# State steps of 64 tokens from chunk 6 on, with k and v loaded by head parity over the partitions

**Chip, cores, metric.** One core of one Trainium2 chip. Times are device microseconds (us) of a whole execution. Most executions of one kernel agree within 1%; some are disturbed and are marked "slow", and comparisons use fast runs alone. The engines: PE is TensorE (PEld its weight loads), DVE VectorE, ACT ScalarE, POOL GpSimd, SP SyncE. A "q" behind a name (SPq) means the engine's instruction queue, which issues DMAs.

## The reference

Linear attention with decay over 4 batches, 8 heads, 768 tokens, head size 64, in blocks of 64 tokens; then an MLP (512 to 2048 to 512) over the 3072 tokens.

```python
Dmask = np.where(rel >= 0, lam[:, None, None] ** rel[None], 0.0)
for b in range(nb):                                  # blocks of 64 tokens
    intra = einsum('bhic,bhjc->bhij', qb, kb) * Dmask
    intra = einsum('bhij,bhjd->bhid', intra, vb)
    inter = einsum('bhid,bhde->bhie', qb * lam_pow, kv_state)
    out[:, :, sl] = intra + inter
    kv_state = lam_block * kv_state + einsum('bhsd,bhse->bhde', kb * rev_pow, vb)
# x: out with the heads side by side, (3072, 512)
h = x @ w_in
g = where(h >= 1, h, where(h <= -1, 0, (h + 1)**2 / 4))
return g @ w_out
```

## The kernel before

A chunk `c` is 128 tokens of one batch with all 8 heads (`C` = 128, `HP` = 4 head pairs, `D` = 64), so there are 24. Six MLP stages of four chunks each follow the attention. PE's two MLP products take most of the time; the attention's work is laid between them.

The order of every engine's instructions is fixed when the program is built: each operation is declared with `add(key, engine, ns, function, needs, due)`, and a list scheduler places them by these assumed durations. At run time each engine then goes through its own list in order.

The operations of one chunk that the change touches:

```python
def f_load(c, x):                      # x: 0 q, 1 k, 2 v; 256 KB, one DMA
    t = qkv_ld[c, x] = ld.tile([128, H, D], F32, ...)      # 6 buffers each
    e = nc.gpsimd if (c, x) > (0, 1) and c < SW else nc.sync
    d = e.dma_start(out=t, in_=(q, k, v)[x][b, :, s0:s0 + C, :].rearrange("h p d -> p h d"))
    ...
def f_xt(c):                           # k and q transposed by the DMA's crossbar
    nc.sync.dma_start_transpose(out=t..., in_=qk[c]...)
def cast_v(c):                         # v times its decay, to bf16
    nc.gpsimd.tensor_tensor(vn[c % NV]..., qkv_ld[c, 2], _bc(tab_k[:, c % NCB, :], 2, D), op=AX.mult)
def f_vb(c, g, hi):                    # v made block-diagonal: 4 small DMAs a chunk
    (nc.gpsimd if c < VP else nc.sync).dma_start(out=vi[c % NV][HD[hi], :, g, hi, :], in_=vn[c % NV][HD[g], :, hi, :])
def f_kb(c, hi):                       # k^T made block-diagonal: 2 DVE copies
    ...nc.vector.tensor_copy(kbd[c % NKB][HD[hi], :, :, hi, :], ptt[c][HD[hi], 0]...)
def f_u(c):                            # state += k^T v, 128 tokens at once
    for hp in range(HP):
        nc.tensor.matmul(pu[0][:, hp, :], lhsT=pair(ks[c], hp), rhs=vn[c % NV][:, hp]..., ...)
def f_s(c, g):                         # scores: 128 columns for g = 0, 64 for g = 1
    ...nc.tensor.matmul(pst[c, g][:, hp, :], lhsT=kbd[c % NKB][:, hp, g]..., rhs=qT[c][:, hp, 64 * g:], ...)
# the load as the scheduler knows it (sp: on the SyncE queue):
add(key, "SP" if sp else "POOL", 600 if sp and i == 0 else 1050 if sp else 900 ..., fn, need, due=0, ...)
```

Of the kernel before, what the change touches and what calls it, by code (L numbers as in the profile page):

```python
# [23 lines left out]
def kernel(  # L24
# [31 lines left out]
    PLAIN, KA = 4, 1  # L56
    LD, RING = 6, 6
# [6 lines left out]
    NQK, NXT, XT = 4, 2, 8  # L64
    qkp = ctx.enter_context(tc.tile_pool(name="qkp", bufs=NQK))
# [37 lines left out]
    NKB, NUB, NV = 3, 3, 4  # L103
    kbd = [const.tile([128, HP, 2, 2, D], BF16, name=f"kbd{i}") for i in range(NKB)]
    ubd = [const.tile([128, HP, 128], BF16, name=f"ubd{i}") for i in range(NUB)]
    vi = [const.tile([128, HP, 2, 2, D], BF16, name=f"vi{i}") for i in range(NV)]
    vn = [const.tile([128, HP, 2, D], BF16, name=f"vn{i}") for i in range(NV)]
# [17 lines left out]
    causal = const.tile([128, 128], F32)  # L125
    plain = const.tile([128, 128], F32)
    for t, p in ((plain, pos[:, 0:1]), (causal, late)):
        nc.vector.tensor_tensor(t, row[:, 0:128], _bc(p, 1, 128).rearrange("p a b -> p (a b)") if False else p.to_broadcast([128, 128]), op=AX.is_ge)
# [11 lines left out]
    tab_k = const.tile([128, NCB, H], F32)  # L140
    tab_q = const.tile([128, NCB, HP, 128], F32)
# [5 lines left out]
    const.tile([128, 56], F32, name="pad1")  # L147
# [28 lines left out]
    def run_plan(free):  # L176
# [25 lines left out]
        while len(out_seq) < len(ops):  # L202
# [4 lines left out]
            if e == "DVE" and t < pool_end:  # L207
                if x.key[0] == "g1" or x.key[0] == "kb" and x.key[1] >= XT:
                    ns += pool_end - t
                elif x.key[0] in ("g2", "g"):  # L210
                    ns += min(ns, (pool_end - t) / 2)
# [5 lines left out]
            for u in users[x.key]:  # L217
                left[u.key] -= 1
                if left[u.key] == 0:
                    lat = SLACK if u.eng == "PE" and x.end > 30000 else DSLACK if u.eng == "SP" else LAT  # L220
                    rel = o_due(u.key[1]) - (14000 if u.key[0] == "t" else 18000) if u.key[0] in ("t", "xt") and u.key[1] >= CPS else o_due(u.key[1]) - 30000 if u.key[0] == "li" and u.key[1] > SW else 0
                    ready[u.eng].append((max([rel] + [y.t if y.eng == u.eng else y.end + lat for y in u.needs]), u))
# [16 lines left out]
    qk, qs, ks, qT, sc_sb, xT, ptt, pst, pot = {}, {}, {}, {}, {}, {}, {}, {}, {}  # L239
# [6 lines left out]
    def cast(c, x, e):  # L246
        if c not in qk:
            qk[c] = qkp.tile([128, 2, H, D], BF16, name="qk", tag="qk")
            ks[c], qs[c] = qk[c][:, 0], qk[c][:, 1]
        t = qk[c][:, 1 - x]  # L250
        if e == "ACT":
            nc.scalar.copy(out=t, in_=qkv_ld[c, x])  # L252
        else:
            nc.vector.tensor_tensor(t, qkv_ld[c, x], qkv_ld[c, x], op=AX.max)

    def f_xt(c):
        t = xtp.tile([128, 2, HP, 128], BF16, name="xq", tag="xq")
        ptt[c] = t
        nc.sync.dma_start_transpose(out=t.rearrange("p a h k -> p (a h) k"), in_=qk[c].rearrange("p a h d -> p (a h d)"))

    def cast_v(c):
        nc.gpsimd.tensor_tensor(vn[c % NV].rearrange("p a b d -> p (a b) d"), qkv_ld[c, 2],  # L262
                                _bc(tab_k[:, c % NCB, :], 2, D), op=AX.mult)

    VP = 24

    def f_vb(c, g, hi):
        o, i = vi[c % NV][HD[hi], :, g, hi, :], vn[c % NV][HD[g], :, hi, :]
        (nc.gpsimd if c < VP else nc.sync).dma_start(out=o, in_=i)  # L269

# [6 lines left out]
    def f_kb(c, hi):  # L277
        if c < PLAIN:
            (nc.scalar.copy if c < KA else nc.vector.tensor_copy)(out=kplain(c), in_=ptt[c][:, 0])
        else:  # L280
            nc.vector.tensor_copy(kbd[c % NKB][HD[hi], :, :, hi, :], ptt[c][HD[hi], 0].rearrange("p a (b d) -> p a b d", b=2))

    def kplain(c):
        return kbd[c % NKB][:, 0:2].rearrange("p a b c d -> p (a b c d)").rearrange("p (h k) -> p h k", k=128)
# [5 lines left out]
    def f_u(c):  # L290
        if c % NCB == 0:
            pu[0] = pp_u.tile([128, HP, 128], F32, name="pu", tag="pu")
        for hp in range(HP):
            nc.tensor.matmul(pu[0][:, hp, :], lhsT=pair(ks[c], hp), rhs=vn[c % NV][:, hp].rearrange("p a d -> p (a d)"),  # L294
                             start=(c % NCB == 0 and hp == 0), stop=True, skip_group_check=True)

    def f_ub(c, hi):
        nc.scalar.copy(out=ubd[c % NUB][HD[hi], :, HD[hi]], in_=pu[0][HD[hi], :, HD[hi]])  # L298

    def f_s(c, g):  # L300
        t = pp_s.tile([128, 4, 128], F32, name="ps", tag="ps")
        pst[c, g] = t if g == 0 or c < PLAIN else t[:, 0:2, :].rearrange("p a (b d) -> p (a b) d", b=2)
        for i in range(4 if c < PLAIN else 0):
            nc.tensor.matmul(t[:, i, :], lhsT=kplain(c)[HD[g], i, :], rhs=qT[c][HD[g], i, :], start=True, stop=True)
        for hp in range(HP if c >= PLAIN else 0):
            nc.tensor.matmul(pst[c, g][:, hp, :], lhsT=kbd[c % NKB][:, hp, g].rearrange("p a d -> p (a d)"),  # L306
                             rhs=qT[c][:, hp, 64 * g:], start=True, stop=True)

    def f_m(c, g):
        if c < PLAIN:  # L310
            t = scp.tile([128, HP, 128], BF16, name="sc128", tag="sc128")
            sc_sb[c] = sc_sb.get(c, []) + [t]
            nc.vector.tensor_tensor(t, pst[c, g], _bc(plain, 1, HP), op=AX.mult)
            return
        if g == 0:
            sc_sb[c] = [scp.tile([128, HP, n], BF16, name=f"sc{n}", tag=f"sc{n}") for n in (128, 64)]
        nc.vector.tensor_tensor(sc_sb[c][g], pst[c, g], _bc(causal[:, 0:128 - 64 * g], 1, HP), op=AX.mult)  # L317

    def f_o(c):
        cb = c % NCB  # L320
        po = pot[c] = pp_o.tile([128, HP, 128], F32, name="po", tag="po")
        for hp in range(HP):
            if cb > 0:
                nc.tensor.matmul(po[:, hp], lhsT=ubd[(c - 1) % NUB][:, hp, :], rhs=qT[c][:, hp, :],  # L324
                                 start=True, stop=False)
            for hi in range(2 if c < PLAIN else 0):
                nc.tensor.matmul(po[HD[hi], hp], lhsT=vn[c % NV][:, hp, hi, :], rhs=sc_sb[c][hi][:, hp, :],
                                 start=(cb == 0), stop=True)
            for g in range(2 if c >= PLAIN else 0):
                nc.tensor.matmul(po[:, hp, 64 * g:], lhsT=vi[c % NV][:, hp, g].rearrange("p a d -> p (a d)"),  # L330
                                 rhs=sc_sb[c][g][:, hp, :], start=(cb == 0 and g == 0), stop=(g == 1))
# [66 lines left out]
    T0, STEP, LEAD = 24000, 1015, 3000  # L398
# [25 lines left out]
    def f_load(c, x):  # L424
        t = qkv_ld[c, x] = ld.tile([128, H, D], F32, name=f"x{x}f", tag=f"x{x}f")
        b, s0 = c // NCB, (c % NCB) * C
        e = nc.gpsimd if (c, x) > (0, 1) and c < SW else nc.sync
        d = e.dma_start(out=t, in_=(q, k, v)[x][b, :, s0:s0 + C, :].rearrange("h p d -> p h d"))  # L428
        if c == SW and x == 1:
            tc.add_manual_dep(d.ins, w_dma[7].ins.name, SYNC)  # L430

    SW = 7
    order = [("c", 0), ("c", 1), ("w", 0), ("c", 2), ("w", 1), ("c", 3), ("w", 2), ("w", 3), ("c", 4), ("w", 4), ("w", 5), ("w", 6), ("c", 5), ("c", 6), ("w", 7)]
    order += [("c", c) for c in range(7, NCH)]

    fifo, landed, splast = [], [], []
    for kind, i in order:
        for x in (1, 0, 2) if kind == "c" else (0,):
            sp = kind == "c" and not (0 < i < SW or (i, x) == (0, 2))
            if kind == "w":  # L440
                key, land, ns, fn, need = ("wi", i), ("w", i), 2800, lambda i=i: load_w(i), []
            else:
                key, land, ns, fn = ("li", i, x), ("ld", i, x), 1060 if sp else 720 if i < 2 else 800, lambda i=i, x=x: f_load(i, x)
                need = [("cast", i - LD, x), ("w", 7) if i == SW else None]
# [7 lines left out]
            add(key, "SP" if sp else "POOL", 600 if sp and i == 0 else 1050 if sp else 900 if kind == "c" else 800, fn, need, due=0, extra=1250 if sp else 930)  # L452
# [3 lines left out]
    for i in range(NKB):  # L456
        last = max(c for c in range(PLAIN) if c % NKB == i)
        add(("z", "kb", i), "DVE", 485, lambda i=i: nc.vector.memset(flat(kbd[i]), 0.0), [("s", last, 1)])
    for i in range(NV):
        add(("zv", i), "POOL", 530, lambda i=i: nc.gpsimd.memset(flat(vi[i]), 0.0), [("cast", 1, 2)], due=10 + i)  # L460
    add(("tabk",), "ACT", 250, lambda: nc.scalar.activation(out=tab_k, in_=arg, func=AF.Exp, scale=-1.0))

    for c in range(NCH):
        od, cb = o_due(c), c % NCB
        lastu = c - 1 if cb else c - 2
        for x in (1, 0):
            e = "DVE" if c == 0 else "ACT"
            add(("cast", c, x), e, 690 if e == "DVE" else 615, lambda c=c, x=x, e=e: cast(c, x, e),
                [("ld", c, x), ("t", c - NQK), ("xt", c - NQK), ("u", c - NQK if (c - NQK) % NCB < NCB - 1 else c - NQK - 1), ("cast", c - 1, x)],
                due=od - 16000 if c >= XT else None)  # L470
        for hp in range(HP) if c < NCB and c % 2 == 0 else ():
            add(("tab", c, hp), "ACT", 410, lambda c=c, hp=hp: tabq(c, hp), [("tab", c, hp - 1), (None, ("kb", 0, 0), ("x", 1))[c // 2]])
        add(("cast", c, 2), "POOL", 1060, lambda c=c: cast_v(c),
            [("ld", c, 2), ("tabk",), ("o", c - NV), ("u", c - NV), ("cast", c - 1, 2)], due=-1)
        for i in range(4 if c >= PLAIN else 0):
            need = [("cast", c, 2), ("o", c - NV), ("zv", c % NV)]
            if c < VP:
# [83 lines left out]
```

## Time and profile before

| | before |
|---|---|
| time, median of 3 runs | 221.31 us (221.18 to 221.66) |
| span of the profiled execution | 220.2 us |
| first 19.6 us | until a slice of weights lands |
| from there to PE's end | 196.9 us |
| tail after PE | 3.7 us |

The busy shares, the chain and PE's timeline are shown and read in the prediction. How to read the table: PE is never idle for long after 19.6 us (its longest stall is 1.0 us), so the time is what PE has to do there. The queue that issues DMAs (SP) is not in the page's busy table, since issuing is not counted as busy.

### The profile page before, as it was taken

To read this page: it belongs to the slowest core of one execution; us is meant where nothing else is said; L and a number is where in the kernel's file an instruction comes from. 1 tells how busy PE (TensorE), PEld (TensorE's weight loads), DVE (VectorE), ACT (ScalarE), POOL (GpSimd) and SP (SyncE) were. 2 spreads that over 40 slices of the span, in tenths; PEclk is the share of its full clock that TensorE was granted. 3 is DMA by queue.
4 is the path that set the end of the run, shared out by engine and by line. 5 is a ranking of instruction groups with operands and counts; after the bars stand their busy time and mean duration, and the time that the engine had idled before them with its cause. 6 is when DMAs were issued, how large, how long until landed. Compare 5 with 4: busy or idle time off the path is not lost.

```text
span 220.2 us, 5365 instructions
## 1 busy us (share of the span) xinstructions
PE 210.5 (96%) x2147; PEld 152.2 (69%) x2180; DVE 154.8 (70%) x276; ACT 136.2 (62%) x249; POOL 103.7 (47%) x143
## 2 busy tenths in 40 slices
PE   7897999989999999999999999999999999999993
PEld 2566788866787858978877677767677776766441
DVE  6543888999499695998999887687668657364200
ACT  6766685655689558677867667755755753554121
POOL 8999874972588545746664357336060000000000
PEclk9999999999999999999999999999999999999999
DMA  5999999959999999989878895796533110110112
GB/s 139 237 239 234 264 209 233 191 98 249 252 245 206 254 226 272 196 223 228 166 186 210 208 209 141 185 212 166 148 75 99 48 47 3 48 48 33 67 57 86
DMA packets 83945, 36.54 MB, mean 166 GB/s; under 512 B 74256, under 2 KB 78352, under 8 KB 83920
## 3 DMA queue, kind: packets, MB, share of 16 engines
q1 hardware_dynamic: 75472, 24.39, 47.6%
q0 software_dynamic: 8304, 11.80, 23.8%
q8 instruction: 17, 0.28, 0.5%
q14 instruction: 8, 0.07, 0.1%
q10 hardware_dynamic: 144, 0.00, 0.0%
HBM read 27.27 MB, written 6.29 MB: 152 GB/s over the span
## 4 chain that ended last, share of the span: by engine, by line
PE 81%; DVE 8%; POOL 5%; DMA 4%; issue 1%; ACT 0%; POOLq 0%; ACTq 0%
PE py L386 35%; PE ph L347 34%; DMA w_in_sb<-in_moe_w_in_dram 4%; PE ps L306 3%; PE po L330 3%; DVE w L365 2%; PE po L324 2%; PE pu L294 2%; DVE gT L380 2%; DVE t L361 2%; POOL x2f L428 1%; POOL vn L262 1%; PE pt L275 1%; DVE sc L317 1%; POOL x1f L428 1%
## 5 line engine op out<-in xcount | busy, mean ns | idle before, releaser
L347 PE MATMUL ph<-xT,w_in_sb 128*128 128x128 bf16 (+1 forms) x1152 | 98.9, 237 | 1.1 <-DMA w_in_sb<-in_moe_w_in_dram 1.1
L355 ACT ACTIVATE r<-ph,one 128x512 bf16<-128x512 f32 x96 | 65.6, 687 | 53.0 <-PE ph L347 41.1
L386 PE MATMUL py<-w_out_sb,gT 128*128 128x512 bf16 x354 | 90.0, 379 | 1.5
L347 PEld LDWEIGHTS <-w_in_sb 128*128 128x128 bf16 x1152 | 80.5, 98 | 12.4 <-DMA w_in_sb<-in_moe_w_in_dram 1.3
L386 PEld LDWEIGHTS <-gT 128*128 128x128 bf16 x384 | 35.8, 98 | 28.7
L269 POOL DMA_DIRECT2D vi<-vn x80 | 50.2, 644 | 10.2 <-POOL vn L262 6.2
L262 POOL TENSOR_TENSOR vn<-x2f,tab_k 128x512 bf16<-128x512 f32 x24 | 27.4, 1140 | 46.0 <-DMA x2f<-in_v_dram 33.2
L361 DVE TENSOR_SCALAR t<-r 128x1024 bf16<-128x1024 bf16 x48 | 27.5, 572 | 28.6 <-ACT r L355 28.6
L365 DVE TENSOR_TENSOR w<-r,t 128x1024 bf16<-128x1024 bf16 x48 | 36.9, 769 | 1.2
L380 DVE TENSOR_TENSOR gT<-w,t 128x1024 bf16<-128x1024 bf16 x48 | 35.3, 735 | 0.9
L317 DVE TENSOR_TENSOR sc<-ps,causal 128x512 bf16<-128x512 f32 (+1 forms) x40 | 22.1, 553 | 5.7 <-PE ps L306 5.4
L391 ACT COPY osb<-py 128x512 f32<-128x512 f32 x24 | 14.1, 586 | 13.9 <-PE py L386 13.1
L337 ACT CAST xT<-po 128x512 bf16<-128x512 f32 x24 | 14.0, 584 | 9.1 <-PE po L330 7.6
L298 ACT CAST ubd<-pu 64x256 bf16<-64x256 f32 x40 | 14.6, 364 | 1.6 <-PE pu L294 1.4
L306 PEld LDWEIGHTS <-kbd 128*128 128x128 bf16 x160 | 10.8, 98 | 6.9 <-issue 0.9
L252 ACT CAST qk<-x0f 128x512 bf16<-128x512 f32 x23 | 14.1, 615 | 0.7 <-DMA x0f<-in_q_dram 0.6
L306 PE MATMUL ps<-qT,kbd 128*128 128x128 bf16 (+1 forms) x160 | 13.3, 206 | 1.0 <-DVE qT L288 0.8
L252 ACT CAST qk<-x1f 128x512 bf16<-128x512 f32 x23 | 14.1, 613 | 0.0
L324 PE MATMUL po<-qT,ubd 128*128 128x128 bf16 x80 | 13.6, 221 | 0.0
L330 PE MATMUL po<-sc,vi 128*128 128x128 bf16 (+1 forms) x160 | 12.9, 206 | 0.0
L229 PE MATMUL py<-idle 128*128 128x512 bf16 x33 | 10.8, 464 | 1.5 <-DVE one L117 1.2
L330 PEld LDWEIGHTS <-vi 128*128 128x128 bf16 x160 | 11.1, 98 | 1.4
(50 smaller groups left out, 122.9 us busy)
## 6 DMA issues: line engine op xcount, KB each, us to landing
out_dram<-osb SPq DMA_DIRECT2D x24, 256.0 KB, 2.2
x1f<-in_k_dram SPq DMA_DIRECT2D x18, 256.0 KB, 3.8
x0f<-in_q_dram SPq DMA_DIRECT2D x18, 256.0 KB, 4.2
x2f<-in_v_dram SPq DMA_DIRECT2D x17, 256.0 KB, 4.5
vi<-vn POOLq DMA_DIRECT2D x80, 32.0 KB, 3.6
w_in_sb<-in_moe_w_in_dram POOLq DMA_DIRECT2D x4, 512.0 KB, 8.3
w_out_sb<-in_moe_w_out_dram POOLq DMA_DIRECT2D x4, 512.0 KB, 9.5
x2f<-in_v_dram POOLq DMA_DIRECT2D x7, 256.0 KB, 4.9
```

Source lines behind the costliest of these rows:

```text
L252: nc.scalar.copy(out=t, in_=qkv_ld[c, x])
L262: nc.gpsimd.tensor_tensor(vn[c % NV].rearrange("p a b d -> p (a b) d"), qkv_ld[c, 2], _bc(tab_k[:, c % NCB, :], 2, D), op=AX.mult)
L269: (nc.gpsimd if c < VP else nc.sync).dma_start(out=o, in_=i)
L306: nc.tensor.matmul(pst[c, g][:, hp, :], lhsT=kbd[c % NKB][:, hp, g].rearrange("p a d -> p (a d)"), rhs=qT[c][:, hp, 64 * g:], start=True, ...
L317: nc.vector.tensor_tensor(sc_sb[c][g], pst[c, g], _bc(causal[:, 0:128 - 64 * g], 1, HP), op=AX.mult)
L330: nc.tensor.matmul(po[:, hp, 64 * g:], lhsT=vi[c % NV][:, hp, g].rearrange("p a d -> p (a d)"), rhs=sc_sb[c][g][:, hp, :], start=(cb == 0 ...
L347: nc.tensor.matmul(ph[:, j * m:(j + 1) * m], lhsT=w_in_sb[:, ko, (i + j) * 128:(i + j + 1) * 128], rhs=xT[s][:, ko, p * m:(p + 1) * m], st ...
L355: nc.scalar.activation(out=r_t[grp][:, i, :], in_=ph_t[s, ni, part], func=AF.Relu, bias=one[:, 0:1])
L361: nc.vector.tensor_scalar(t_t[grp], r_t[grp], 0.5, 1.0, op0=AX.mult, op1=AX.min)
L365: nc.vector.tensor_tensor(w_t[grp], r_t[grp], t_t[grp], op=AX.subtract)
L380: nc.vector.tensor_tensor(o, w, t, op=AX.mult)
L386: nc.tensor.matmul(py_t[s, ms], lhsT=gT[s][:, ko, ms * 128:(ms + 1) * 128], rhs=w_out_sb[:, ko, :], start=(ko == 0), stop=(ko == FO - 1))
```

## The change

Its intent: less work for PE and DVE. With state steps of 64 tokens, the scores need only the diagonal blocks, 64 columns for each head instead of 128 and 64. For this, even heads' tokens must lie on other partitions than odd heads': k and v are loaded so that partition p holds, of one 64-token half, the four even or the four odd heads. Two copies then place k into a tile `kq` with zeros, and one crossbar transpose of `kq` (12 blocks instead of 8) yields the block-diagonal k^T directly: the DVE copies of k^T and the four small DMAs of v go. Chunks 0 to 5, not 0 to 3, keep the "plain" form.

```diff
-    PLAIN, KA = 4, 1
+    PLAIN, KA = 6, 1
 def f_load(c, x):
-        d = e.dma_start(out=t, in_=(q, k, v)[x][b, :, s0:s0 + C, :].rearrange("h p d -> p h d"))
+        e = nc.gpsimd if pool_ld(c, x) else nc.sync
+        src = (q, k, v)[x][b, :, s0:s0 + C, :]
+        if c < PLAIN or x == 0:
+            d = [e.dma_start(out=t, in_=src.rearrange("h p d -> p h d"))]
+        else:
+            d = [e.dma_start(out=halves(t)[HD[hi], a], in_=src.rearrange("(h b) (a p) d -> b a p h d", b=2, a=2)[hi, a])
+                 for a in range(2) for hi in range(2)]
+    def f_ki(c, hi):
+        nc.scalar.copy(out=kq[c % NKQ][HD[hi], 0:2 * HP, HD[hi]], in_=qkv_ld[c, 1][HD[hi]])
+    def f_qn(c):
+        nc.vector.tensor_tensor(kq[c % NKQ][:, 2 * HP:, :]..., qkv_ld[c, 0], _bc(tab_n...), op=AX.mult)
 def f_xt(c):
-        nc.sync.dma_start_transpose(out=t..., in_=qk[c]...)
+        nc.sync.dma_start_transpose(out=t, in_=kq[c % NKQ]...)      # 12 blocks
-    def f_vb(c, g, hi):
-        (nc.gpsimd if c < VP else nc.sync).dma_start(out=o, in_=i)
+    def f_vb(c, hi):
+        nc.gpsimd.tensor_copy(vi[c % NV][HD[hi], :, HD[hi]], vn[c % NV][HD[hi]])
-    f_u(c), f_ub(c, hi): one step of 128 tokens
+    f_u(c, j), f_ub(c, j, hi): two steps of 64 tokens, j = 0, 1
 f_s, f_o:  (cut)  64-column matmuls, one for each half and head pair
-            add(key, "SP" if sp else "POOL", 600 if sp and i == 0 else 1050 if sp else 900 ...
+            add(key, "SP" if sp else "POOL", 600 if sp and i == 0 else 1050 if sp and x == 0 else 1500 if sp else 900 ...
     (cut: tables, buffers, needs and due times of the plan)
```

The loads of k and v are now four DMAs of 64 KB each. The new number 1500 is the plan's duration for the four together.

## The prediction

> **What bounds the kernel now.** First the page's busy shares, its slices and its chain.
>
> ```profile
> PE 210.5 (96%) x2147; PEld 152.2 (69%) x2180; DVE 154.8 (70%) x276; ACT 136.2 (62%) x249; POOL 103.7 (47%) x143
> ...
> PE   7897999989999999999999999999999999999993
> ...
> PE 81%; DVE 8%; POOL 5%; DMA 4%; issue 1%; ACT 0%; POOLq 0%; ACTq 0%
> ```
>
> PE is nearly always busy and carries 81% of the chain. A busy PE need not be a full one, so I looked at the starts of matmuls in the timeline of PE (start, duration, group).
>
> ```profile
> 101.25 0.28 PE L306 MATMUL ps<-qT,kbd 128*128 128x64 bf16 x4
> 101.37 1.06 PE L347 MATMUL ph<-xT,w_in_sb 128*128 128x128 bf16 x16
> ...
> 103.35 0.50 PE L330 MATMUL po<-sc,vi 128*128 128x128 bf16 x8
> ```
>
> One 128-column matmul lasts 219 ns, one of 64 columns 193 ns (groups by form). Sixteen of 128 columns end 1.06 us after the first starts: (1060-219)/15 = 56 ns from start to start. Four of 64: (280-193)/3 = 29 ns. The eight of L330 alternate 128 and 64 columns: (500-193)/7 = 44 ns, the mean of the two. So PE's time is matmul columns, each matmul has its own weight load hidden behind it, and half the columns cost half the time. One exception stands in the early stretch.
>
> ```profile
> 19.63 1.07 PE L347 MATMUL ph<-xT,w_in_sb 128*128 128x128 bf16 x16 [1.12 <-DMA w_in_sb<-in_moe_w_in_dram]
> 20.63 0.40 PE L304 MATMUL ps<-qT,kbd 64*128 64x128 bf16 x4
> 20.96 0.40 PE L294 MATMUL pu<-vn,qk 128*128 128x128 bf16 x4
> ...
> 24.05 0.23 PE L324 MATMUL po<-qT,ubd 128*128 128x128 bf16 x1
> 24.21 0.25 PE L327 MATMUL po<-sc,vn 128*64 128x128 bf16 x2
> 24.39 0.23 PE L324 MATMUL po<-qT,ubd 128*128 128x128 bf16 x1
> ```
>
> Up to 19.63 us PE waits for a slice of weights, whatever it did before. After that I count. The four half-array matmuls of L304 cost 0.33 us from 20.63 to 20.96, plus the late start after the last matmul ahead (20.48 in the record, so 0.15 instead of 0.056): about 0.20 us more than 4 x 56 ns. In the output step of a "plain" chunk (0 to 3) L324 uses the whole array and L327 half of it; they alternate with a period of 0.34 us per head pair, against 0.11 for the two starts. Each change of array shape costs about 0.1 us.
>
> Last, PE's waits.
>
> ```profile
> PE ph L347 <- DMA w_in_sb<-in_moe_w_in_dram: 1.1, 1, 1.1
> PE ps L306 <- DVE qT L288: 0.8, 1, 0.8
> ```
>
> Adding up matmuls from 19.63 us by these spacings gives 195.1 us; PE really ends at 216.5, 196.9 later. Only 1.75 us is stall: 1.0 at 47.6 us (the line above, counted from start to start), and 0.32, 0.15 and 0.28 us at 22.4, 67 and 94. The tail after PE is 3.7 us. So from 19.6 us on the time is the number of PE columns and of shape changes, plus what the new schedule stalls.
>
> **What the Trainium skill says.** "TensorE: Matmul & The Clock Gate", section "Back-to-back issue gap", gives N/2.4+2.5 ns for a warm matmul: 55.8 ns at 128 and 29.2 ns at 64. The trace has 56 and 29. The same section speaks of about 81 ns per matmul of 128 columns in a stream with weight loads; this trace does not show that, and I use the trace. "TensorEngine Tiling (Array Packing)", section "Key Properties", says that changing the tiling mode drains the engine; the 0.1 us per change agrees. "SBUF — State Buffer", section "SBUF: two separate sides", says VectorE instructions in a two-port mode or with two SBUF inputs, and GpSimd instructions, take a shared port pair exclusively and block one another. The trace agrees: L361 takes 0.42 us alone and beside a POOL DMA issue (median of each), but 0.73 (median) and up to 1.27 beside the multiplication vn on POOL.
>
> **The change part by part, on PE.** Chunks 0 to 5 are now plain, 6 to 23 work in two steps of 64 tokens with block-diagonal k and v. I counted matmuls from the two programs' orders, from the first matmul after the weight wait.
>
> Before: 128 columns, whole array: 40 transposes, 72 state, 80 scores, 76 inter-chunk output, 80 output = 348 x 56 ns = 19.5 us. 64 columns: 160 x 29 = 4.6. Half-array scores: 16 x 56 = 0.9, with 4 groups of shape changes at 0.2 = 0.8. L327: 8 concurrent pairs x 56 = 0.45, with 8 alternations at 0.23 = 1.8. Together 28.1 us.
>
> After: 24 transposes, 8 state and 16 inter-chunk matmuls of 128 columns: 48 x 56 = 2.7. 64 columns: 132 state, 144 scores, 132 inter-chunk, 144 output = 552 x 29 = 16.0. Half-array scores, two more plain chunks: 32 x 56 = 1.8, with 8 groups x 0.2 = 1.6. Output of four plain chunks: 16 pairs x 56 = 0.9, and since the new order does all inter-chunk matmuls first, one entry and exit per chunk, 4 x 0.21 = 0.8. Together 23.8 us.
>
> That is -4.3 us. The fillers that the program puts in while it expects to wait go from 6 to 8 after 19.6 us (8 x 0.216 against 6): +0.4. The two MLP products do not change (736 + 384 + 384 matmuls). So PE's path gives 3.9 us; by unrounded spacings I get 3.6, and I use 3.7. The work falls from 448,000 to 438,784 columns, 3.84 us at 2.4 GHz: most of the gain.
>
> **Beside the path.** DVE: away go 40 block copies of k (9.8+3.3 us), 18 queries from the transposed tile become 18 before it at about the same 0.69 us, scores change from 20 x (0.69+0.42) + 8 x 0.69 = 27.7 to 30 x 0.69 = 20.7. With small additions, about -18 us of 154.8. ACT: 40 state copies of 0.364 us become 76 (+13.1), casts stay (46 x 0.615 against 10 + 36): about 150 us of 217, not the bound. POOL: 80 DMA issues (50.2 us) become 36 copies 64x512. A one-input instruction on the same width, the memset, takes 0.57 us; my estimate is 0.6 to 0.8, so about 25 us. But these copies take the shared port, which issues did not, so DVE loses some of what it gains. SP: k and v loads are four DMAs each; the shortest issue seen is 0.36 us, so some 1.5 us per tile, and per chunk about 2 x 1.5 + 0.6 + 1.9 (transpose, 1.3 x 12/8) + 0.4 = 5.9 us, where one stage of four chunks takes about 32 us, 8 each. The transfers of vi vanish, the transposed tiles grow by half.
>
> **Rivals.** (1) A new stall eats the gain. For it: in the stretch 40 to 50 us DVE was busy 9.78 of 10 us, which made the 1.0 us stall; new plain chunks 4 and 5 have fuller masks, and POOL will block DVE more:
>
> ```profile
> 43.66 2.35 DVE L365 TENSOR_TENSOR w<-r,t 128x1024 bf16<-128x1024 bf16 x1
> 44.39 1.06 POOL L262 TENSOR_TENSOR vn<-x2f,tab_k 128x512 bf16<-128x512 f32 x1
> ```
>
> Against: after 50 us DVE has slack that grows. I summed DVE from there to chunk 5's scores: 26.0 us before, 26.5 after, with one MLP step and one query scaling more in the second figure; chunk 5 should come a little easier. If it fails, +1 to +3 us: 218.5 to 220.5. (2) State steps in series: each chunk now goes PE, two ACT copies (0.73 us), PE, copies, twice. The order of PE has 1.7 us or more of MLP work between the steps, so two copies and one activation (0.69) fit; if ACT comes late by 0.2 us per chunk, 18 x 0.2 = +3.6 us, and no gain is left. (3) The k/v loads or the longer transpose starve later chunks: DMA share was 1.05 in 50 to 100 us. Against: tile loads run six chunks ahead and PE never waited for one; +2 us if wrong. (4) The 1.75 us of stalls goes away with DVE's relief: 215.8. (5) Long runs of 64-column matmuls can't hide weight loads; 4 ns more on 552 would be +2.2. Runs of four and alternating eights show no such sign.
>
> **Range and chances.** 221.3 - 3.7 = 217.6; I expect 1.0 to 1.2 us of stalls instead of 1.75, mainly because chunk 5's query is earlier in DVE's order: 217.0. The line of 2% is 216.9, so faster and same are nearly even. Stalls gone gives 215.8; one rival of +2 gives 219. Range 215.5 to 219.0; faster 0.46, same 0.50, slower 0.04.
>
> **What would show it.** Right: 64-column matmuls of scores, state and output start 29 ns apart in runs of 8 and 16; PE starts the MLP's third group at about 19.6 us and ends near 213; the plain output shows one change of shape, not eight; PE's waits total under 1.5 us; vi copies on POOL of 0.6 to 0.8 us, with L361's counterpart slower on average than its 572 ns. Wrong: a PE wait above 1 us on DVE at 40 to 55 us, repeated waits for the state copies on ACT, waits for the transposed tile, or 64-column spacing above 31 ns.

## The result, and the profile after

| | before | changed |
|---|---|---|
| median | 221.49 us (221.18 to 222.05, 4 runs) | 248.45 us (246.1 to 552.5, 4 runs) |
| ratio of fast runs | | 1.1125 [1.1075, 1.1175] |

A ratio is the mean time of one kernel's fast runs over that of the other's fast runs of the same rounds, so it is not quite the ratio of the medians. The changed kernel is 11% slower; 217.0 with a range of 215.5 to 219.0 was predicted. Two of its four runs count as slow (552.5 and 250.06); the two fast ones took 246.1 and 246.85.

The profile that came with this result fell in the run of 552.5 us. Is it of any use? The first work of PE, eleven filler matmuls that both kernels have, answers that. Timeline of PE (start, duration, group), the changed kernel in that execution:

```profile
1.19 6.54 PE L238 MATMUL py<-idle 128*128 128x512 bf16 x11 [1.19 <-DVE one L118]
```

and the kernel before:

```profile
1.19 4.87 PE L229 MATMUL py<-idle 128*128 128x512 bf16 x11 [1.19 <-DVE one L117]
```

The same eleven matmuls took 6.54 us instead of 4.87 (4.39 in the fast profile of the changed kernel that comes next). That execution was disturbed as a whole. I leave it out, and why PE was slow in it stays open (its granted clock is recorded as 1.0). All that follows reads "the changed kernel" from a new profile of it, the first experiment (a fast run, 244.49 us).

Its page: busy shares, slices of PE, and the chain, which follows the work that ended last back through whatever released it.

```profile
PE 210.4 (87%) x2277; PEld 147.5 (61%) x2312; DVE 146.4 (60%) x234; ACT 150.3 (62%) x287; POOL 81.2 (33%) x96
...
PE   7799979999987969778979778888869999999993
...
PE 39%; DMA 19%; SPq 17%; ACT 7%; DVE 7%; issue 5%; POOL 4%; ACTq 0%; POOLq 0%; DVEq 0%
```

PE's busy time is what it was, but over a longer span: 87% instead of 96%, with holes from the twelfth slice to the thirtieth and full again after. PE carries 39% of the chain, where it had 81%. The rest went to DMA and to "SPq", the queue of SyncE, which had no share in the chain before. No compute engine got fuller. So PE's holes come from waits, at the end of which stands a DMA or its issue. The chain of waits (for what, us in total, times, longest):

```profile
POOL vn L280 <- DMA x2f<-in_v_dram: 93.6, 19, 7.6
...
PE pu L311 <- POOL vn L280: 10.6, 9, 2.0
```

PE waits for vn, POOL's product with v, and POOL waits for the load of v: 93.6 us in total, 33.2 in the kernel before. Idle POOL alone costs nothing, but nine of these waits reach PE. The loads of k weigh at least as much: by line, they have 7% of the chain, those of v 4%.

Is the load slow to move, or late to start? The median from issue to landing, from the page's list of DMA issues, is 2.6 to 2.8 us for a 64 KB load, and was 3.8 to 4.5 for 256 KB before. So each lands sooner, once issued. A whole tile doesn't: from the first of its four issues to the last landing it takes a median of 4.6 us for k and 5.0 for v. The issues themselves by line (count, duration ns min/median/max, first and last start us), before:

```profile
L428 SPq DMA_DIRECT2D x1f<-in_k_dram x18: 367/574/1127, 0.7 to 151.3; - x18
...
L428 SPq DMA_DIRECT2D x2f<-in_v_dram x17: 376/923/2240, 49.6 to 157.2; - x17
```

and the changed kernel:

```profile
L452 SPq DMA_DIRECT2D x1f<-in_k_dram x72: 595/615/1354, 38.1 to 188.5; - x72
L452 SPq DMA_DIRECT2D x2f<-in_v_dram x72: 595/615/1425, 41.6 to 191.9; - x72
```

The 144 issues take a median of 615 ns each, at the least 595. The first k issue is at 38.1 us, the last chunk's first at about 188.5 - 3 x 0.65 = 186.5: 148.4 us for 17 chunks, 8.7 us each. PE has work for 191.4/24 = 8.0 us a chunk (195.1 - 3.7 of the prediction). The loads come more slowly than PE could use them, and a lead of some chunks only delays the moment when it feels that.

The timeline of SP shows what fills the 8.7 us; the kernel before has waits and gaps between its issues:

```profile
111.50 1.24 SPq L259 DMA_TRANSPOSE xq<-qk  x1
112.80 0.57 SPq L428 DMA_DIRECT2D x1f<-in_k_dram  x1
113.42 0.57 SPq L428 DMA_DIRECT2D x0f<-in_q_dram  x1
114.09 1.48 SPq L428 DMA_DIRECT2D x2f<-in_v_dram  x1
117.81 1.24 SPq L259 DMA_TRANSPOSE xq<-qk  x1
```

and the changed kernel has next to none:

```profile
79.50 1.51 SPq L275 DMA_TRANSPOSE xq<-kq  x1
81.10 2.58 SPq L452 DMA_DIRECT2D x1f<-in_k_dram  x4
83.78 0.55 SPq L450 DMA_DIRECT2D x0f<-in_q_dram  x1
84.46 2.61 SPq L452 DMA_DIRECT2D x2f<-in_v_dram  x4
87.17 1.31 SPq L415 DMA_DIRECT2D out_dram<-osb  x1
```

From one row to the next about 0.1 us passes. The v load issued from 84.46 to 87.07 is the one that POOL waits for at 89.57, and PE behind it (timelines of POOL and PE):

```profile
89.57 1.54 POOL L280 TENSOR_TENSOR vn<-x2f,tab_v 128x512 bf16<-128x512 f32 x1 [5.03 <-DMA x2f<-in_v_dram]
```

```profile
91.17 0.28 PE L311 MATMUL pu<-vn,kq 128*128 128x64 bf16 x4 [1.95 <-POOL vn L280]
```

In the stretch from 55 to 190 us (135 us) I added the records of SP: 123.2 us of issues and 10.6 us in gaps under 0.2 us between them, so 133.8 of 135 us. Before it was 70.1 and 4.5, the rest longer waits. SP is full, and in that stretch PE is busy for 112.9 of 135 us.

### The profile page after: what moved, and what is told of

Same layout as the page of the kernel before. It is cut to its first block, busy times and chain, and to the rows that moved or that the text cites. A ratio compares the mean times of both kernels' runs of the same rounds, so it can differ in the third digit from the quotient of the medians.

```text
span 550.7 us, 5754 instructions
## 1 busy us (share of the span) xinstructions
PE 545.7 (99%) x2312; PEld 304.8 (55%) x2312; DVE 135.8 (25%) x234; ACT 153.6 (28%) x287; POOL 74.2 (13%) x96
## 4 chain that ended last, share of the span: by engine, by line
PE 99%; ACT 0%; DVE 0%; issue 0%; ACTq 0%
PE py L406 42%; PE ph L367 41%; PE py L238 4%; PE pu L311 2%; PE ps L323 2%; PE po L350 2%; PE po L348 2%; PE ps L320 1%; PE pt L289 1%; PE po L342 1%; PE po L338 1%; DVE qT L297 0%; ACT kT L293 0%; ACT osb L411 0%; DVE idle L95 0%
## 5 line engine op out<-in xcount | busy, mean ns | idle before, releaser
L367 PE MATMUL ph<-xT,w_in_sb 128*128 128x128 bf16 (+1 forms) x1152 | 244.5, 435 | 0.0
L406 PE MATMUL py<-w_out_sb,gT 128*128 128x512 bf16 x384 | 242.4, 835 | 0.0
L367 PEld LDWEIGHTS <-w_in_sb 128*128 128x128 bf16 x1152 | 170.0, 172 | 76.2 <-issue 33.1
L406 PEld LDWEIGHTS <-gT 128*128 128x128 bf16 x384 | 63.8, 172 | 111.9 <-issue 105.4
L381 DVE TENSOR_SCALAR t<-r 128x1024 bf16<-128x1024 bf16 x48 | 22.3, 464 | 203.1 <-ACT r L375 203.1
L280 POOL TENSOR_TENSOR vn<-x2f,tab_v 128x512 bf16<-128x512 f32 x18 | 18.8, 1042 | 307.6 <-DMA x2f<-in_v_dram 272.5
L400 DVE TENSOR_TENSOR gT<-w,t 128x1024 bf16<-128x1024 bf16 x48 | 34.9, 727 | 1.3
L283 POOL COPY vi<-vn 64x512 bf16<-64x512 bf16 x36 | 25.4, 706 | 1.9
L350 PE MATMUL po<-sc,vi 128*128 128x64 bf16 x144 | 23.4, 283 | 0.0
L348 PE MATMUL po<-xq,ubd 128*128 128x64 bf16 x132 | 22.8, 288 | 0.0
L266 ACT CAST kq<-x1f 64x512 bf16<-64x512 f32 x36 | 22.1, 613 | 0.6
L348 PEld LDWEIGHTS <-ubd 128*128 128x128 bf16 x132 | 17.1, 149 | 3.5 <-issue 3.2
```

What stands on the lines that cost most here:

```text
L283: nc.gpsimd.tensor_copy(vi[c % NV][HD[hi], :, HD[hi]], vn[c % NV][HD[hi]])
L348: nc.tensor.matmul(po[:, hp, HD[j]], lhsT=ubd[(2 * c + j - 1) % NUB][:, hp, :], rhs=qT[c][:, hp, HD[j]], start=True, stop=False)
L350: nc.tensor.matmul(po[:, hp, HD[j]], lhsT=vi[c % NV][:, HP * j + hp, :], rhs=sc_sb[c, 1][:, hp, HD[j]], start=(cb == 0 and j == 0), stop=True)
L367: nc.tensor.matmul(ph[:, j * m:(j + 1) * m], lhsT=w_in_sb[:, ko, (i + j) * 128:(i + j + 1) * 128], rhs=xT[s][:, ko, p * m:(p + 1) * m], st ...
L400: nc.vector.tensor_tensor(o, w, t, op=AX.mult)
L406: nc.tensor.matmul(py_t[s, ms], lhsT=gT[s][:, ko, ms * 128:(ms + 1) * 128], rhs=w_out_sb[:, ko, :], start=(ko == 0), stop=(ko == FO - 1))
```

## The experiments

Theory S: SP's time for issuing is the bound, because each of the eight small issues a chunk costs 0.6 us, and not the transfers, the order of PE or the 64-token steps. Its rivals, as the expectations below word them, are above all a disturbance that is not the kernel's, slower 64-column matmuls, the transfers themselves, and the order in which the plan puts SP's issues. Letters in an expectation are those that it defines itself. The medians of the kernel before are those of the same job. Medians and ranges take in the slow runs (one in c_plan_2600, 239.65, and one in d_p5_g5, 223.18), the ratios do not.

| label | median (range) us | before us | ratio [95%] | result |
|---|---|---|---|---|
| a1_again | 245.34 (244.33 to 246.2) | 221.86 | 1.1069 [1.0987, 1.1151] | correct |
| b_one_issue | 218.18 (217.81 to 219.06) | 221.27 | 0.9868 [0.9821, 0.9915] | wrong |
| b_ten_issues | 254.07 (253.06 to 255.3) | 221.27 | 1.1487 [1.1426, 1.1548] | correct |
| b_v_pool | 217.26 (217.13 to 217.91) | 221.27 | 0.9826 [0.9784, 0.9869] | correct |
| b_v_act | 245.44 (244.73 to 245.82) | 221.27 | 1.1095 [1.1035, 1.1154] | correct |
| c_head_quarters | 226.22 (224.37 to 226.79) | 221.41 | 1.0218 [1.0145, 1.0291] | wrong |
| c_plan_2600 | 236.1 (234.93 to 239.65) | 221.41 | 1.0662 [1.0571, 1.0752] | correct |
| d_p5_g5 | 219.86 (219.33 to 223.18) | 221.41 | 0.9937 [0.987, 1.0003] | correct |
| d_p4_g4 | 221.84 (221.36 to 223.98) | 221.41 | 1.0065 [0.9975, 1.0155] | correct |
| e_v_pool_plan | 270.5 (269.59 to 271.78) | 220.92 | 1.222 [1.2166, 1.2273] | correct |
| e_v_pool_ahead | 219.01 (218.4 to 219.05) | 221.29 | 0.9898 [0.9845, 0.995] | correct |

**a1_again.** No edit: the changed kernel once more, in three rounds.

> The changed kernel itself, unchanged, because the only trace of it fell in a disturbed execution: there even the first eleven filler matmuls, which both kernels share, start 485 to 621 ns apart instead of 430, so PE was held back from the first microsecond on, whatever the kernel. Theory A (the kernel itself is slow): 244 to 250 us again, 1.10 to 1.13 of the kernel before, and a profile with full-speed matmuls (56 ns at 128 columns) but about 28 us of PE waits. Theory B (the chip was disturbed for this kernel's executions alone): 215 to 219 us, 0.97 to 0.99. Theory C (the 64-column matmuls can't hide their weight loads): 244 to 250 us with few waits, and 552 matmuls of 64 columns spaced about 29 + 28000/552 = 80 ns instead of 29.

245.34 us: the 11% are the kernel's. The matmuls run at full speed (the 64-column ones start 29 ns apart), and PE waits.

**b_one_issue.** k and v in one DMA each, in the plain layout. The result is wrong (relative error 0.095), since heads and tokens lie on other partitions than the rest assumes; all the same instructions run on the same amount of data.

```diff
-            d = [e.dma_start(out=halves(t)[HD[hi], a], in_=src...[hi, a]) for a in range(2) for hi in range(2)]
+            d = [e.dma_start(out=t, in_=src.rearrange("h p d -> p h d"))]
```

> k and v of chunks 6 to 23 are each loaded by one 256 KB DMA, as in the kernel before, instead of four of 64 KB; nothing else changes, also not the order of instructions. The result is wrong on purpose (the heads then lie in the wrong partitions). Theory S (SP can't issue fast enough: 0.62 us per issue plus 0.04 between, eight for k and v in each chunk): SP gets back 6 x 0.65 = 3.9 us per chunk, PE is the bound again: 216 to 218 us. Theory T (the transfers of 64 partitions are slow or crowd the DMA engines): also faster, but this run does not tell it from S. Theory Z (ACT's state copies, POOL's copies or the longer transpose cost the time): 238 to 245 us.

218.18 us, 27 us less than the changed kernel, with its bytes, its plan and its order left as they were. SP's issues from 55 to 190 us fall to 67.9 us.

**b_ten_issues.** The other direction: q too in two DMAs, one more issue a chunk, and nothing else.

```diff
+        elif x == 0:
+            d = [e.dma_start(out=t[HD[i]], in_=src[:, HD[i]].rearrange("h p d -> p h d")) for i in range(2)]
```

> Chunks 6 to 23 load q by two DMAs of 64 partitions instead of one; ten issues for loads in a chunk instead of nine; the same bytes, right result. Theory S: 0.65 us more on SP in each of the some 16 chunks during which SP is the bound: +8 to +12 us on 244.5, so 252 to 257. Theory T: the bytes and rows are the same, so 243 to 248. Theory Z: 243 to 246.

254.07 us: 8.7 us more for 18 more issues, 0.48 us each. With SP full (123.3 us of issues and 10.6 of small gaps in the stretch), an added issue goes for the most part into the time: q's two halves have a median of 0.633 us each, the whole tile had 0.603.

**b_v_pool.** All transfers stay as in the changed kernel, but POOL, which is busy for 33%, issues the loads of v. The result is correct.

```diff
-        e = nc.gpsimd if pool_ld(c, x) else nc.sync
+        e = nc.gpsimd if pool_ld(c, x) or x == 2 else nc.sync
```

> v of chunks 6 to 23 keeps its four DMAs but POOL issues them instead of SP; right result. Theory S: SP gets back 2.6 us per chunk: 217 to 223, less than all if POOL (4 x 0.92 us more per chunk) or the shared port with DVE comes into the way. Theory T: the same transfers, so 240 to 248. Theory Z: 240 to 250.

217.26 us. This tells S from the transfers: the same 144 DMAs of the same shape run, and the 28 us are gone. One difference in the transfers has to be looked at: by the packet counts of the DMA queues, POOL's queue moves the 72 loads of v in 2,304 packets, SP's in 19,584. They don't land sooner for it: the median to landing is 3.3 us, for k too, where it was 2.6 to 2.8. And in c_head_quarters below, bytes and packets are as many as in the changed kernel, the issues are shorter, and 19 us go. Busy shares and chain of b_v_pool's page:

```profile
PE 208.6 (97%) x2312; PEld 147.4 (68%) x2312; DVE 149.2 (69%) x234; ACT 150.1 (70%) x287; POOL 125.5 (58%) x168
...
PE 88%; DMA 4%; DVE 3%; POOL 2%; ACT 1%; issue 0%; POOLq 0%; ACTq 0%
```

PE carries 88% of the chain and SPq nothing. Its issues by line and eight scores in PE's timeline:

```profile
L452 SPq DMA_DIRECT2D x1f<-in_k_dram x72: 596/616/1627, 36.8 to 154.8; - x72
L452 POOL DMA_DIRECT2D x2f<-in_v_dram x72: 617/621/734, 40.2 to 157.7; - x72
```

```profile
102.22 0.40 PE L323 MATMUL ps<-xq 128*128 128x64 bf16 x8
```

An issue costs the same as before the edit on SP, and 0.62 us on POOL. But the k loads of a chunk now come every (154.8 - 1.9 - 36.8)/17 = 6.8 us, under PE's 8.0. The eight matmuls start (400 - 193)/7 = 29.6 ns apart. The Trainium skill, "DMA: Bandwidth & Descriptors", section "Issuing engines are not separate DMA queues", says that issuing from several engines saves only the sequencer's time to initiate a DMA. This run agrees. It adds that this time "is usually small relative to the DMA itself"; here it was 0.615 us against 2.6 to landing, and the bound.

**b_v_act.** The same with ACT's queue instead of POOL's.

```diff
+        e = nc.gpsimd if pool_ld(c, x) else (nc.scalar if c >= PLAIN and x == 2 else nc.sync)
```

> v of chunks 6 to 23 keeps its four DMAs but ACT issues them instead of SP; right result. Theory S: 217 to 226; ACT gets some 72 x 0.6 = 43 us of issues and would be near 90% of the span, so it may become a second bound. Theory T: 240 to 248. Theory Z (ACT too slow already): above 250.

245.44 us, a miss of S as I had put it. SP is relieved as much, but ACT's stream runs in order too. Timelines of ACT and PE:

```profile
91.47 2.85 ACTq L452 DMA_DIRECT2D x2f<-in_v_dram  x3
94.37 0.37 ACT L314 CAST ubd<-pu 64x256 bf16<-64x256 f32 x1 [2.75 <-issue]
```

```profile
94.79 0.29 PE L311 MATMUL pu<-vn,kq 128*128 128x64 bf16 x4 [1.41 <-ACT ubd L314]
```

The second copy of the state stands behind three issues for 2.75 us, and PE's next state step waits for it. Waits of this kind add up to 12.0 us on PE, 4.7 in the changed kernel; with those for ACT's other work it is 19.5 of the 25.5 us that PE waits in this run. Issues must go where nothing urgent stands behind them: POOL was such a place, ACT was not.

**c_head_quarters.** Is it the number of issues or their shape? Four DMAs of 64 KB again, but each over 128 partitions with two heads, instead of 64 with four. Its output is wrong, which doesn't matter for the time.

```diff
+            d = [e.dma_start(out=t[:, 2*i:2*i+2], in_=src[2*i:2*i+2].rearrange("h p d -> p h d")) for i in range(4)]
```

> k and v of chunks 6 to 23 are again loaded by four DMAs of 64 KB each on SP, but each takes two heads over all 128 partitions instead of four heads over 64 partitions; wrong result on purpose. It measures whether the 0.615 us of an issue belong to any DMA or to the form over 64 partitions. Theory S1 (an issue costs about 0.6 us whatever its shape): issues of 0.6 us, 242 to 248 us. Theory S2 (the form over half the partitions is slow, one over all 128 costs 0.36 us, the shortest seen in the kernel before): issues of 0.36 to 0.45 us, SP gets back about 8 x 0.2 = 1.6 us of 8.4 per chunk, 217 to 222 us.

226.22 us, between the two cases of the expectation:

```profile
L452 SPq DMA_DIRECT2D x1f<-in_k_dram x72: 368/468/1177, 37.2 to 170.0; - x72
```

The same bytes and the same number of rows cost a median of 468 ns instead of 615 for each issue. So the shape counts beside the number: 8 x 0.147 = 1.2 us a chunk. The minima say more, since a median also holds what an issue waits for: over 64 partitions an issue took at least 595 ns, with four heads (k, v) as with eight (q in b_ten_issues); over 128 partitions at least 368 with two heads, and 367 to 390 with eight (the whole tiles of the two kernels). So on SP it goes with the partitions, 64 being dearer than 128, and not with the bytes. It is no queue of earlier issues: in b_v_act six issues of k came after more than 0.5 us without an issue on SP, and took a median of 595 ns. On POOL the order is the other way round: 0.62 us for 64 KB over 64 partitions, and at least 0.88 for a whole tile. Why, these runs don't show. A version with two DMAs a tile was not run.

**c_plan_2600.** How much does the order cost that comes from the plan's wrong 1500 ns?

```diff
-  ... 1050 if sp and x == 0 else 1500 if sp else 900 ...
+  ... 1050 if sp and x == 0 else 2600 if sp else 900 ...
```

> The changed kernel, but its own plan is told that the four issues of k or v take SP 2600 ns (measured: 4 x 0.62 + 3 x 0.04) instead of 1500, so the order on all engines is made anew. Right result. Theory P (SP could keep up, only the order is bad): 217 to 225 us. Theory S (nine loads, one transpose and one store take SP 8.4 us per chunk, whatever the order, and PE's work leaves about 8): 235 to 246 us.

236.1 us, 9 us better than the changed kernel and still 15 us worse than before. SP is as full as it was: 121.3 us of issues and 11.0 of small gaps from 55 to 190 us. But it has left the chain, and PE now waits for other things, since the order on all engines has moved with that one number (chain, then two of PE's waits):

```profile
PE 71%; ACT 8%; DVE 7%; DMA 5%; POOL 4%; issue 3%; SPq 0%; ACTq 0%; POOLq 0%
...
PE py L406 <- DVE gT L400: 6.5, 5, 1.8
PE po L350 <- DVE sc L330: 2.9, 3, 1.4
```

So of the 24 us a truthful plan gives back some 9; what in its order does so was not tested. How much of the other 15 is SP's pace, and how much the new order's waits for DVE and ACT, this run doesn't tell. In the old order it is plainer: there, relieving SP alone is worth 28 (b_v_pool).

**d_p5_g5, d_p4_g4.** Can b_v_pool be bettered by fewer plain chunks, which cost more columns and shape changes? Both have v on POOL, with `PLAIN` 5 and 4, the weights' gate (`GATE`) moved to 5 and 4, the list of loads shortened to match, and in the second the memsets' needs fitted (the diff is cut).

```diff
-    PLAIN, KA = 6, 1
+    PLAIN, KA = 5, 1        # 4 in the other
-    GATE = {SW: 6}
+    GATE = {SW: 5}          # 4 in the other
```

> An attempt at a better version: v issued on POOL as in the run before, and the step of 64 tokens from chunk 5 on, whose loads wait for the sixth slice of weights instead of the seventh. Right result. A plain chunk takes PE about 2.2 us, one of the new kind 0.9, so PE saves 1.2 us: 216.0 us, if the loads and the transpose of chunk 5 come in time; if not, PE waits in 45 to 55 us and the time is 217 to 219.

> The same from chunk 4 on, gated by the fifth slice of weights. PE would save 2.5 us: 214.8 us; but the plan already puts twenty matmuls of the second product in a row before chunk 4's state, which shows that it expects the data late: more likely a PE wait of some us at 40 to 55 us, 217 to 222.

219.86 and 221.84 us: no gain. In the second, PE waits four times for about 1 us between 54 and 63 us, twice each for ACT and DVE: there the columns saved come back as waits in the early chunks. In the first no such waits stand early: its PE takes 193.2 us from the third group of the MLP to its end, where b_v_pool takes 192.4, with one wait of 0.8 us at 74.6. Why it is no faster stays open. Six plain chunks, as the change has it, did best.

**e_v_pool_plan.** If a truthful plan helped SP, does it help b_v_pool? The plan is told that v's loads run on POOL for 2600 ns, k's on SP for 2600 and q's for 700.

```diff
-  add(key, "SP" if sp else "POOL", ... 1050 if sp and x == 0 else 1500 if sp ...
+  add(key, "SP" if sp and (x < 2 or i == 0) else "POOL", ... 700 if sp and x == 0 else 2600 if sp ...
```

> v issued on POOL as before, and the kernel's own plan told so: 2600 ns of POOL for v, 2600 ns of SP for k, 700 for q. Right result. If what is left over PE's columns is stalls from a wrong order, the time falls from 217.3 to at most 216.5, since that run had 0.7 us of PE stalls above 0.13 us each after 19 us; if the order was good enough, 216.5 to 218, the same within noise.

270.5 us, the worst of all and a large miss. POOL's timeline:

```profile
54.05 1.60 POOL L283 COPY vi<-vn 64x512 bf16<-64x512 bf16 x2
55.60 2.47 POOL L452 DMA_DIRECT2D x2f<-in_v_dram  x4
60.60 1.54 POOL L280 TENSOR_TENSOR vn<-x2f,tab_v 128x512 bf16<-128x512 f32 x1 [2.53 <-DMA x2f<-in_v_dram]
```

A load is issued only when the copies of the chunk ahead are done, and the next product waits for it. That looks like a lost lead, and I took it for the cause. The record speaks against it. In b_v_pool, too, POOL's product starts 0.2 us after its own load has landed, in 17 of 18 chunks. And POOL is not late here: its product with v ends a median of 42 us before the chunk's output step begins on PE (17 us in b_v_pool). POOL waits for PE rather than PE for POOL (waits of POOL and PE):

```profile
POOL vi L283 <- PE po L350: 23.0, 10, 4.6
...
PE py L406 <- DVE gT L400: 14.9, 14, 1.9
PE po L350 <- DVE sc L330: 9.6, 9, 2.2
...
PE pu L311 <- POOL vn L280: 0.3, 1, 0.3
```

So the plan has made a new order on all engines, and PE waits for DVE and ACT in it. Which move in that order costs the 50 us stays open. The granted clock of its six runs was lower too, 0.956 to 0.974 where b_v_pool's had 0.998 to 1.0. Even if all of the time went with the clock, that would be some 4%, 11 us by this estimate.

**e_v_pool_ahead.** The same truthful plan, but v's loads are freed from the chain with q's and given the earliest due time, so that they run ahead.

```diff
-            elif i:
+            elif i and x < 2:
-            if sp:
+            if sp and x < 2:
-  ... fn, need, due=0, ...
+  ... fn, need, due=-2 if sp and x == 2 and i >= PLAIN else 0, ...
```

> As in the run e_v_pool_plan, but v's loads no longer wait in the plan for q's of the same chunk and go first on POOL, so that several of them stand ahead of the multiplications that use them, instead of one right after each chunk's copies. Right result. If the missing lead of v's loads made that run slow (each chunk there shows 2.5 us of issues, a wait of 2 to 4 us for landing, then 2.7 us of work on POOL, one after another): 216 to 222 us. If not (the new order is bad in other ways, on ACT or DVE): above 235 us, and the cause of that run's 270 stays open.

219.01 us: where the plan places v's loads decides. But this edit, too, makes the order of all engines anew, so it doesn't show that the lead at run time was what was missing, as the expectation has it. Here the loads do run ahead, the products starting 1.0 to 9.3 us after their landing, and that brings nothing: it is no better than b_v_pool, which stays the best version: correct, and faster than both kernels (0.9826 of the time before; its interval lies below 1, but 2% is not shown).

## Why the prediction was wrong, by its own steps

**The step that failed** is the term for SP in the part "beside the path": "k and v loads are four DMAs each; the shortest issue seen is 0.36 us, so some 1.5 us per tile, and per chunk ... = 5.9 us, where one stage of four chunks takes about 32 us, 8 each." Four issues took 2.58 to 2.61 us, not 1.5. With them the chunk's issues add up to 2.58 + 0.55 + 2.61 + 1.51 (transpose) + 0.5 (store) and some 0.5 us between them, 8.3 us, and the loads came every 8.7. The limit of 8.0 that I had set beside it was right, so a right number in that place would have turned the forecast. Two mistakes made it wrong. I took the minimum, although the view of before that I had gives a median of 574 ns for k: 4 x 0.574 is 2.3 us, which alone makes 7.5 us a chunk and leaves no room. And I took the figure of a 256 KB tile over 128 partitions for issues of 64 KB over 64, a shape that SP doesn't issue in the trace of before; measured, it is the dearer one, at the least 595 ns against 367. For the transpose I had 1.9 us and for the store 0.4; they were 1.51 and 0.52.

**Rival 3 was dismissed on the wrong ground.** "Tile loads run six chunks ahead and PE never waited for one": a lead covers late loads, not loads that come more slowly than they are used. Nor was it six, which is the number of buffers: in the trace of before, when a load of k or v was issued, at most five chunks ahead of it had their output step still to come, and POOL already waited 33.2 us for v. And its cost of +2 us was set for transfers, where the issues cost 28 over the forecast of 217.0.

**What held.** The columns of PE did: with SP relieved, in b_v_pool, the stretch from the third group of the MLP (19.23 us) to PE's end (211.64) takes 192.4 us, where the prediction has 195.1 - 3.7 = 191.4 and 1.0 to 1.2 of stalls. Before it was 196.9. The time of that version is 217.26 against the 217.0 forecast: it describes the change without its issues. Rival 5 (64-column matmuls that can't hide the weight loads) fell at 29.6 ns, and rival 2 (late state copies) cost nothing in b_v_pool, 4.7 us of PE's waits in the changed kernel and 12.0 where ACT issues DMAs. Rival 1 (a new stall) didn't come either: after 19.6 us b_v_pool's PE waits for DVE once, 0.2 us at 35.0. The plain output has one change of shape a chunk, as forecast. ACT was 150.3 us against "about 150". The copies of vi took 0.80 us on average (0.82 in b_v_pool), the top of 0.6 to 0.8.

**Sizes that were off without effect.** DVE lost 8.4 us (5.6 in b_v_pool), where about 18 were predicted, less something for the shared port. L400, the last product, went from a mean of 735 ns to 860: the 13 of its 48 that run beside POOL's product with v took a median of 1.41 us, the 24 that run beside nothing on POOL 0.69. L381, the counterpart of L361, was not slower than 572 ns in the changed kernel (555), and barely in b_v_pool (580). One reading was off: of the L361 beside vn the prediction's 0.73 and 1.27 us leave out the longest, 1.83 us at 40.0; the median of all 14 is 0.96.

**Not settled.** The 552.5 us run; why an issue over 64 partitions costs more than one over 128; what in the order makes e_v_pool_plan slow; how the rest of c_plan_2600's loss divides.

## What to carry to other kernels

An engine that only issues DMAs has a budget like any other: count issues in each period, multiply by the median of the same shape (not the minimum, and not scaled by bytes), and set the sum beside the period of the bound engine. A prefetch lead hides latency, never a shortage of rate. When issues move to another engine, look for what stands behind them in its order, and check what order a scheduler makes of it: the same 72 issues gave 217 us on POOL, 245 on ACT, and 270 on POOL with the plan made anew.

The Trainium skill names the pattern: "Perfetto Trace Analysis", section "What "DMA-bound" means", lists as a bound of its own the issuing engine's sequencer, whose track is then solid DMA slices, and says that this time is descriptor generation, not data movement. The trace agrees: 133.8 of 135 us of SP, while the DMA engines' mean busy share in the same stretch was 0.74, under the 0.76 of before.

## What the Trainium skill lacked or had wrong

- "DMA: Bandwidth & Descriptors", section "Issuing engines are not separate DMA queues": the time to initiate is called usually small. Here it bounded the kernel, and the page has no figure in time by shape for this chip. The runs show medians of 0.615 us on SP for 64 KB over 64 partitions and four heads, 0.468 for 64 KB over 128 partitions and two heads, 0.574 for a whole 256 KB tile of k, 1.51 for the transpose of 12 blocks, and 0.621 on POOL for the first of these; the least on SP was 0.595 over 64 partitions and 0.367 over 128.
- The same page, section "Rules for kernel authors", advises against two transfers to disjoint halves of the partitions, because they share the same engines. The advice holds here, but there is a cost that the row does not give: the issues, which make the 27 us between b_one_issue and the changed kernel. Whether the halves also hold each other up, as the row says, was not tested; a whole tile of k landed 4.6 us after its first issue, 3.8 before.
- "TensorE: Matmul & The Clock Gate", section "Back-to-back issue gap": its 81 ns for matmuls of 128 columns in a stream with weight loads is not what these traces show (56 ns), and 64 columns with weight loads ran at 29.6 ns.
